# Retention chunks 0 to 5 turned in TensorE's transpose mode, their loads spread over three DMA queues, and another order of the first steps

## The chip, the cores and the metric

The kernel runs on one core of a Trainium2 chip. The metric is the device time of one execution in microseconds (us). The time before is a median of 667.78 us over 8 runs (666.61 to 669.93).

A core has five engines that run side by side, each with its own queue of instructions in a fixed order: TensorE (PE; its weight loads are listed apart as PEld), VectorE (DVE), ScalarE (ACT), GpSimd (POOL) and SyncE (SP). SP, ACT and POOL can issue DMA transfers between the chip's memory (HBM) and the on-chip buffers; a DMA that SP or ACT issues and one that POOL issues appear in the profile under different queues. An instruction that waits holds up everything behind it in its own queue.

## What is computed

The reference is a recurrent retention block (4 batches, 8 heads, 768 steps, head dimension 64), whose output is reshaped to 3072 x 512 and goes through a two-layer network with a quick GELU between:

```python
gamma = 1.0 - 2.0 ** (-5.0 - np.arange(H))
for t in range(S):
    state = gamma * state + einsum('bhd,bhe->bhde', k[:, :, t], v[:, :, t])
    y[:, :, t] = scale * einsum('bhd,bhde->bhe', q[:, :, t], state)
x = y.transpose(0, 2, 1, 3).reshape(B * S, H * D)      # 3072 x 512
h = x @ w_in                                           # 512 -> 2048
g = h * (1.0 / (1.0 + np.exp(-1.702 * h)))
out = g @ w_out                                        # 2048 -> 512
```

The two weights are handed to the kernel as raw 64-bit words (8 bytes for each value) and are narrowed to 32-bit floats on the chip.

## The kernel before, in words

**Retention.** The sequence is cut into chunks of 64 steps; two batches are worked on together (one in partitions 0 to 63, the other in 64 to 127), so there are 24 chunk steps j, 12 for each pair of batches. For a step, `load` (L125) brings q, k and v in tiles of 128 partitions x 8 heads x 64; `turn` (L239) makes the transposes of q and k; `turned` (L257) copies them out of PSUM on ACT; `attend(j, f)` (L280, called "step j-f") makes k·q products of chunk j (L288) and, for an earlier chunk f, the state's update (L296) and the output from the state (L305) and from the chunk itself (L311); `masked` (L315, DVE) applies the decay mask; `decay` (L262, ACT, eight instructions at L271) scales k; `by_state` and `output` (L320, L332, DVE) write the chunk into X; `aged` (ACT) and `updated` (DVE, L367) carry the state.

In steps 0 to 5 (`NEW = 6`) `turn` uses TensorE: 16 ordinary products of a 128 x 64 weight (two heads' halves go to the two halves of the output's partitions) with the identity matrix as the moving operand (L249). From step 6 on DVE's own transpose does it.

**The network.** X feeds products with w_in: the first two blocks (`up0` at L413, `up1` at L426), whose weights are narrowed while the kernel runs; later blocks use sums of weight and activation tiles that save products (L471, L575, L708).

**Narrowing a weight tile** ("w3" and so on, L180 to L220). SP fetches two 512 KB halves "b" and "a" into one of three raw buffers (`fetch`, L176, DMA at L178); ACT takes `abs` (L205); DVE does `half` (L209 to L211, 2.6 us for a full tile) and `rest` (L215 to L220, 3.2 us). A raw buffer is free for the tile after next but one when `rest` is done.

**The order.** PE's instructions stand in the order in which the program is written. On the other engines most of the first part is pinned to program order too. For the first stage that order is a list of words at L844 to L860, walked one after the other: `k0` is "load k of step 0", `turn0`, `w0b` is "fetch half b of weight tile 0", `abs0b`, `half0b`, `rest0b` narrow it, `step1` or `step5-4` is `attend`, `x0` writes the output of chunk 0, `up0.0.3` a product of the network, `gate0.0.3` its GELU, `warm` (L760) a product of the identity matrix with itself. `begin` (L749) comes ahead of the list; `rows` (L765), `mask` (L807), `causal` (L770, two instructions on POOL) build the decay mask, `whole` (L780) and `halves_anew` (L791) load and lay out decay factors. All DMAs of q, k and v are issued by SP, but k of step 0 by ACT. A tile of q, k or v has two buffers.

In the built program the DMAs of SP and ACT together take turns on eight completion semaphores, and those of POOL on eight others: a DMA waits until the one eight places ahead of it has landed.

```python
def plain(name, src, tag, bufs, engine=sp):                              # L133
    t = two.tile([P, H, D], F32, name=name + "_in", tag=tag, bufs=bufs)
    for i in range(2):
        if j < NEW:
            keep(engine.dma_start(t[i * D:(i + 1) * D], src[b + i, :, rows, :].rearrange("h p d -> p h d")))
...
for r in range(2):                                                       # L248
    pe.matmul(p[n][HALF[r], s, :], x[n][:, HP * r + s, :], ident, start=True, stop=True)
```

Of the kernel before, what the change touches and what calls it, by code (L numbers as in the profile page):

```python
# [9 lines left out]
F32 = mybir.dt.float32  # L10
U32 = mybir.dt.uint32
AF = mybir.ActivationFunctionType
ALU = mybir.AluOpType
P = 128
# [14 lines left out]
def kernel(  # L29
# [28 lines left out]
    nc = tc.nc  # L58
    pe, act, dve, pool, sp = nc.tensor, nc.scalar, nc.vector, nc.gpsimd, nc.sync
    ctx.enter_context(tc.manual_schedule(engines={mybir.EngineType.PE}))  # L60

    B, H, S, D = q.shape
    NT, DM = out.shape
    DFF = moe_w_in.shape[1]
    HP = H // 2
# [13 lines left out]
    one = ctx.enter_context(tc.tile_pool(name="one", bufs=1))  # L79
    two = ctx.enter_context(tc.tile_pool(name="two", bufs=2))  # L80
# [20 lines left out]
    rowd = const.tile([P, HP, D], F32, name="rowd")  # L101
    row = G[0:1, 4, 0:2].rearrange("p a (h t) -> p (a h) t", t=D)
    ones = G[0:1, 4, 2, 0:P]
    cold = const.tile([P, 2 * H], F32, name="cold")
    whole = const.tile([P, HP], F32, name="whole")
    whole_h = const.tile([P, H], F32, name="whole_h")
    ident = const.tile([P, P], F32, name="ident")
    mask = const.tile([P, 2, HP, D], F32, name="mask")
# [9 lines left out]
    def pin(i):  # L118
        return tc.keep_in_program_order(i) if ordered[0] else i


    NEW = 6
    QKV = {}

    def load(j, what="qkv"):  # L125

        b, c = j // NC * 2, j % NC
        rows = slice(c * D, (c + 1) * D)  # L130
        keep = tc.keep_in_program_order if j < 2 * CB else lambda i: i

        def plain(name, src, tag, bufs, engine=sp):  # L133
            t = two.tile([P, H, D], F32, name=name + "_in", tag=tag, bufs=bufs)
            QKV[name, j] = t
            for i in range(2):
                if j < NEW:
                    keep(engine.dma_start(t[i * D:(i + 1) * D], src[b + i, :, rows, :].rearrange("h p d -> p h d")))
                else:
                    for r in range(2):  # L140
                        keep(engine.dma_start(t[r * D:(r + 1) * D, i * HP:(i + 1) * HP],
                                              src[b + i, r * HP:(r + 1) * HP, rows, :].rearrange("h p d -> p h d")))

        if j < NEW:
            if "q" in what:
                plain("q", q, "q_sq", 2)
            if "k" in what:
                plain("kn", k, "k_sq", 2, sp if j else act)
        elif "q" in what:
            for name, src in (("q", q), ("k", k)):  # L150
                t = two.tile([P, H, D // C4, C4], F32, name=name + "_sq")
                for r0 in range(0, P, C4):
                    for n in range(D // C4):
                        t0 = c * D + n * C4
                        tc.keep_in_program_order(sp.dma_start(  # L155
                            t[r0:r0 + C4, :, n], src[b + r0 // D, :, t0:t0 + C4, r0 % D:r0 % D + C4]
                            .rearrange("h p d -> p h d")))
                QKV[name, j] = t
        if "v" in what:
            if j >= NEW and c < NC - 1:  # L160
                plain("kn", k, "kn", 1)
            plain("v", v, "v", 2)


    w1v = moe_w_in.bitcast(U32).rearrange("(c p) (f two) -> p c f two", p=P, two=2)
# [59 lines left out]
    QT, KT, KD, AT, TURNED, PA, PU, PY, SHARE = [{} for _ in range(9)]  # L225
    HALF = [slice(i * D, (i + 1) * D) for i in range(2)]
# [12 lines left out]
    def turn(j):  # L239

        QT[j], KT[j] = home(j, "qT"), home(j, "kT")
        if j < NEW:

            x = QKV.pop(("q", j)), QKV["kn", j]
            TURNED[j] = p = [ps.tile([P, HP, P], F32, name="pt", tag="y") for i in range(2)]
            for n in (1, 0) if j else (0, 1):
                for s in range(HP):
                    for r in range(2):  # L248
                        pe.matmul(p[n][HALF[r], s, :], x[n][:, HP * r + s, :], ident, start=True, stop=True)  # L249
        else:  # L250
            for t, name in ((QT[j], "q"), (KT[j], "k")):
                tc.keep_in_program_order(dve.transpose(
                    t.rearrange("p h t -> p (h t)"), QKV.pop((name, j)).rearrange("p h n d -> p (h n d)")))
        if 2 * CB <= j < NCH - 2:
            load(j + 2, "qk")
# [6 lines left out]
    def decay(j):  # L262

        if j % NC == NC - 1:
            return
        KD[j] = home(j, "kd")
        x = QKV["kn", j]
        if j < NEW:

            for h in range(H):  # L270
                pin(act.activation(KD[j][:, h], x[:, h], AF.Copy, scale=cold[:, H + h:H + h + 1]))  # L271
        else:
            pool.tensor_mul(KD[j].rearrange("p (i s) d -> p i s d", i=2), x.rearrange("p (i s) d -> p i s d", i=2),
                            cold[:, None, H:H + HP, None].to_broadcast([P, 2, HP, D]))
# [468 lines left out]
    W = col_decay.shape[1]  # L743
# [3 lines left out]
    works, products = {}, {}  # L747

    def begin():  # L749
        for i in range(2):  # L750

            pin(pool.dma_start(
                cold[HALF[i]].rearrange("p (n h) -> p n h", n=2),
                bass.AP(tensor=col_decay.tensor, offset=col_decay.offset, ap=[[W, D], [D * W + H, 2], [1, H]])))
        pin(pool.dma_start(row, row_decay[None, :, 0:D]))
        make_identity(nc, ident)
        dve.memset(ones, 1.0)
        dve.memset(first, 0.0)

# [27 lines left out]
    def late_loads():  # L787
        load(2 * CB, "qkv")
        load(2 * CB + 1, "qk")

    def halves_anew():  # L791

        pool.dma_start(whole_h, bass.AP(tensor=col_decay.tensor, offset=col_decay.offset + (D - 1) * W + H,
                                        ap=[[0, P], [1, H]]))
        pool.tensor_copy(mask[HALF[1], 0], mask[HALF[1], 1])
        pool.tensor_copy(cold[HALF[1], H:H + HP], cold[HALF[1], H + HP:2 * H])
        old, new = state[NEW % NC % 2], state[(NEW + 1) % NC % 2]
        for u in range(2):
            pool.dma_start(new[HALF[1 - u], u], old[HALF[u], 1 - u])
        for u in range(2):  # L800
            pool.tensor_copy(old[HALF[u], 1 - u], new[HALF[u], 1 - u])
# [20 lines left out]
    for name, i in [("0a", 0), ("0b", 1)] + [(str(p), 2 * p) for p in range(1, NFF)]:  # L822
        n = Narrow(i)
# [17 lines left out]


    begin()
    for name in """  # L844
        k0 table q0 warm turn0 w0b rows warm k1 abs0b q1 turned0 step0 v0 w0a half0b mask turn1 causal rest0b
        masked0 decay0 v1 decay1 abs0a half0a step-0 updated0 turned1 q2 step1 rowd k2 whole w2b turn2 w2a x0 k3
        aged1 masked1 turned2 v2 rest0a abs2 q3 step-1 updated1 state1 decay2 aged2 step2 q4 x1 half2 decay3 w3b
        w3a up0.0.0 masked2 turn3 k4 step-2 v3 q5 rest2 k5 gate0.0.0 turned3 updated2 state2 step3 up0.0.2
        masked3 abs3 half3 x2 rest3 turn4 w1b step-3 aged3 gate0.0.2 turned4 state3 w1a w5b updated3 v5 decay4
        abs1 x3 turn5 half1 up0.0.3 turned5 up0.1.2 step4 aged4 w5a rest1 v4 gate0.0.3 decay5 w6a masked4  # L850
        gate0.1.2 abs5 w6b step5-4 half5 rest5 up0.0.1 updated4 abs6 state4 gate0.0.1 w4b
        up0.1.1 half6 aged5 w4a up0.0.5 rest6 masked5 up0.1.5 gate0.1.1 x4 gate0.0.5 abs4 step-5 w8b w8a
        half4 gate0.1.5 state5 updated5 anew q6 up0.1.6 x5 rest4 gate0.1.6 abs8 v6 up0.0.6 w7b w7a half8
        turn6 gate0.0.6 up0.1.0 abs7 half7 gate0.1.0 w9b w9a up0.1.4 q7 gate0.1.4 decay6 step6 masked6 rest7 up0.0.4 v7
        gate0.0.4 turn7 up0.1.3 gate0.1.3 aged6 step7-6 masked7 updated6 decay7 abs9 state6 x6 up0.0.7 rest8 gate0.0.7
        w11a w11b step-7 state7 x7 half9 w10b w10a up0.1.7 rest9 gate0.1.7 abs11 half11 up1.8 gate1.8
        w12a w12b rest11 up1.5 gate1.5 up1.4 gate1.4 abs10 half10 up1.0 gate1.0 rest10 up1.3 gate1.3 abs12
        aged7 updated7 up1.2 gate1.2 w14b w14a half12 up1.6 gate1.6 rest12 up1.9 gate1.9 abs14 half14 w13a w13b
        up1.11 gate1.11 rest14 up1.10 gate1.10 abs13 half13 w15a w15b up1.7 gate1.7 rest13 abs15 half15 up1.12
        gate1.12 late_loads up1.13 gate1.13 rest15 up1.15 gate1.15 up1.14 gate1.14 up1.1 gate1.1  # L860
    """.split():
        works[name]()
# [93 lines left out]
```

## Time and profile before

| | |
|---|---|
| median of 8 runs | 667.78 us |
| the profiled execution | 669.93 us, of which the span is 668.2 us |
| mean granted TensorE clock | 0.995 |
| PE busy | 648.9 us (97% of the span) |
| DVE busy | 435.4 us (65%) |
| ACT, POOL busy | 148.8 us (22%), 176.2 us (26%) |
| the turn's products, L249 | 192 records on PE, 273 ns median each, from 6.4 to 44.2 us |
| one turn at full clock | 1.90 us on the chain of waits (at 31.25, 39.09 and 42.55 us) |
| loads of q, k, v of steps 0 to 5 | 12 DMAs each, 128 KB each |
| weight halves, 512 KB each | 5.7 us median from issue to landing (w_in into W) |

The page gives, for each engine, its busy time, then the span in 40 slices of 16.7 us (a digit is the busy share in tenths), then the DMA queues, then the chain of work that ended last, followed back from the end. The timeline lists instructions by start, with the idle time ahead of them and what ended it in brackets; a window query gives each engine's busy time, the granted clock, the DMA engines' busy share and GB/s in a stretch. Times are counted from the start of the span. A transfer's landing is read from the trace's completion events: each of 16 DMA engines reports once, and the transfer is complete with the last of the 16.

### The profile page before, as it was taken

The numbers are of one execution on the slowest core, as the hardware profiler recorded it, in microseconds if no ns is written. First come the engines' busy times: TensorE is split into PE (matmuls) and PEld (weight loads), VectorE is DVE, ScalarE is ACT, GpSimd is POOL, SyncE is SP. The second block draws the span as 40 slices with busy tenths as digits, with TensorE's granted clock in tenths as the row PEclk, the third lists the DMA queues.
The fourth block names the chain that finished last, engine by engine and source line by source line (L and its number), as shares of the span: only waits on it lengthen the run. The fifth ranks groups of instructions, "written<-read, shape, count | busy, mean of one in ns | idle before, by whom it ended". The sixth has DMA issues, their size and how long they took to land.

```text
span 668.2 us, 15234 instructions
## 1 busy us (share of the span) xinstructions
PE 648.9 (97%) x6438; PEld 563.3 (84%) x6438; DVE 435.4 (65%) x618; ACT 148.8 (22%) x285; POOL 176.2 (26%) x196
## 2 busy tenths in 40 slices
PE   6799989999999999999999899999999999999997
PEld 3788875446888888888999788999888999988997
DVE  3698778788545775456985254996264995254965
ACT  5664222231000000233100233110233110233110
POOL 3000310000268326100445600255700255500000
PEclk9799999999999999999999999999999999999999
DMA  9996557452203546263385652276662143502142
GB/s 182 218 228 182 144 106 233 153 98 33 47 10 134 172 111 181 60 224 123 88 216 126 206 143 94 73 178 174 176 177 95 61 148 112 221 32 94 51 157 94
DMA packets 150500, 89.49 MB, mean 134 GB/s; under 512 B 136192, under 2 KB 137472, under 8 KB 149408
## 3 DMA queue, kind: packets, MB, share of 16 engines
q1 hardware_dynamic: 140944, 46.50, 30.5%
q0 software_dynamic: 7184, 40.78, 17.0%
q10 hardware_dynamic: 2304, 1.25, 0.6%
q8 instruction: 50, 0.82, 0.5%
q14 instruction: 18, 0.15, 0.1%
HBM read 72.89 MB, written 15.47 MB: 132 GB/s over the span
## 4 chain that ended last, share of the span: by engine, by line
PE 83%; DMA 7%; SPq 3%; DVE 2%; POOL 2%; issue 1%; ACT 1%; POOLq 0%; DVEq 0%; ACTq 0%
PE pq L575 21%; PE px L471 16%; PE pd L708 13%; PE py L471 12%; PE ph L426 8%; PE ph L413 6%; DMA v_in<-in_v_dram 2%; DMA kn_in<-in_k_dram 2%; PE pa L288 2%; SPq L155 2%; PE pt L249 1%; PE pa L296 1%; PE py L311 1%; DMA W<-in_moe_w_out_dram 1%; PE py L305 1%
## 5 line engine op out<-in xcount | busy, mean ns | idle before, releaser
L575 PE MATMUL pq<-W,G 128*128 128x128 f32 x672 | 80.5, 276 | 0.1
L575 PEld LDWEIGHTS pq<-W,G 128*128 128x128 f32 x672 | 77.6, 192 | 0.9 <-issue 0.3
L544 POOL DMA_DIRECT2D ring<-W2D x28 | 15.4, 551 | 228.2 <-PE px L471 118.0
L471 PE MATMUL px<-X,W1A 128*128 128x256 f32 x256 | 60.0, 380 | 2.8 <-POOL X L441 2.8
L471 PE MATMUL px<-X,W1B 128*128 128x256 f32 x256 | 59.8, 379 | 0.0
L575 PE MATMUL pq<-ring,own 128*128 128x128 f32 x448 | 59.8, 276 | 0.0
L471 PEld LDWEIGHTS px<-X,W1A 128*128 128x128 f32 x256 | 48.2, 190 | 9.9 <-POOL X L441 3.6
L575 PEld LDWEIGHTS pq<-ring,own 128*128 128x128 f32 x448 | 54.5, 192 | 0.4
L471 PEld LDWEIGHTS px<-X,W1B 128*128 128x128 f32 x256 | 48.5, 190 | 6.7
L708 PE MATMUL pd<-W,G 128*128 128x256 f32 x224 | 49.6, 381 | 0.0
L708 PEld LDWEIGHTS pd<-W,G 128*128 128x128 f32 x224 | 42.2, 190 | 5.9
L471 PE MATMUL py<-X,W1A 128*128 128x256 f32 x192 | 45.4, 379 | 0.0
L471 PE MATMUL py<-X,W1B 128*128 128x256 f32 x192 | 45.4, 379 | 0.0
L392 ACT ACTIVATE G<-G 128x512 f32<-128x512 f32 x48 | 30.2, 630 | 52.0 <-DVE G L481 33.4
L471 PEld LDWEIGHTS py<-X,W1A 128*128 128x128 f32 x192 | 36.5, 190 | 5.0
L471 PEld LDWEIGHTS py<-X,W1B 128*128 128x128 f32 x192 | 36.5, 190 | 5.0
L489 DVE TENSOR_TENSOR t<-py,u 128x512 f32<-128x512 f32 x16 | 11.1, 692 | 35.3 <-PE py L471 35.3
L478 ACT ACTIVATE p<-px 128x512 f32<-128x512 f32 x16 | 9.6, 597 | 94.3 <-PE px L471 94.3
L575 PE MATMUL pq<-ring,G 128*128 128x128 f32 x224 | 29.6, 275 | 0.0
L575 PE MATMUL pq<-W,own 128*128 128x128 f32 x224 | 29.6, 275 | 0.0
L413 PE MATMUL ph<-X,W1B 128*128 128x256 f32 x128 | 29.0, 382 | 0.4 <-ACT X L392 0.4
L503 DVE TENSOR_TENSOR G<-G 128x512 f32<-128x512 f32 (+2 forms) x24 | 12.3, 513 | 25.7 <-ACT G L392 25.7
(206 smaller groups left out, 1163.4 us busy)
## 6 DMA issues: line engine op xcount, KB each, us to landing
ring<-W2D POOLq DMA_DIRECT2D x28, 768.0 KB, 5.0
W1B<-W1D POOLq DMA_DIRECT2D x6, 1792.0 KB, 9.5
W<-in_moe_w_in_dram SPq DMA_DIRECT2D x12, 512.0 KB, 5.7
W<-in_moe_w_out_dram SPq DMA_DIRECT2D x10, 512.0 KB, 5.5
out_dram<-o POOLq DMA_DIRECT2D x20, 256.0 KB, 3.5
q_sq<-in_q_dram SPq DMA_DIRECT2D x144, 32.0 KB, 2.4
k_sq<-in_k_dram SPq DMA_DIRECT2D x144, 32.0 KB, 2.4
v_in<-in_v_dram SPq DMA_DIRECT2D x72, 64.0 KB, 3.1
```

What stands on the lines that cost most here:

```text
L155: tc.keep_in_program_order(sp.dma_start(t[r0:r0 + C4, :, n], src[b + r0 // D, :, t0:t0 + C4, r0 % D:r0 % D + C4] .rearrange("h p d -> p h ...
L288: pe.matmul(pa[HALF[w], u, 0, s, :], kt[HALF[u], w, s, :], qt[HALF[u], w, s, :], start=True, stop=True)
L392: pin(act.activation(g, h[:, i], AF.Gelu_apprx_sigmoid))
L413: pe.matmul(h[:, ab], w, X[:, 2 * th + c // 2, c % 2, :], start=(ab == 0 and c == 0), stop=(c == 3), skip_group_check=True)
L426: pe.matmul(h, w, X1[:, c // 2:4:2, c % 2, :], start=(c == 0), stop=(c == 3))
L471: pe.matmul(acc[:, u, :], t[:, q1 + u, sa, c, :], X[:, sb, c, :], start=(start and u == 0 and c == 0), stop=(stop and c == 1), skip_group_ ...
L478: act.activation(p1, x, AF.Copy)
L489: dve.tensor_add(tt, z, u)
L503: dve.tensor_sub(q[0][1], q[0][0], q[0][1])
L544: pool.dma_start(c, W2D[i])
L575: pe.matmul(p0[:, j, :], a[:, d], w[:, d], start=(new and j == 0 and d == 0), stop=(d == NP // 2 - 1), skip_group_check=True)
L708: pe.matmul(p0[:, n, :], g1(m, p, sa)[:, n * P:(n + 1) * P], W2[:, sb, p, :], start=(new and p == 0 and n == 0), stop=(last and p == NP - ...
```

## The change

- `turn` in steps 0 to 5: 8 products in transpose mode, 128 x 128 each (two neighbouring heads at once), in place of 16 products of 128 x 64. So that neighbours are the right pair, q and k are loaded with heads 0 to 3 at the even places of the tile and heads 4 to 7 at the odd ones: four DMAs of 64 KB in place of two of 128 KB. `decay` reads the heads at their new places.
- k is loaded by ACT in step 0, by SP in step 2 and by POOL in steps 1, 3, 4, 5 (before: ACT in step 0, SP in the others). v of steps 0 to 5 is loaded by POOL (before: SP). q stays on SP.
- k of steps 2 and 3 takes the two buffers of the later output tile `o`; v of steps 2 and 3 those of two later scratch tiles (`s1`, `s2`), so that these four loads wait for no earlier step.
- In `begin`, POOL issues the load of `row`, makes the identity matrix and only then issues the loads of `cold`. The load of `whole_h` moves from about 3.4 us to its place in the list, behind all of POOL's other loads of this stage.
- The order of the first words: three `warm` and `rows` before `turn0`; `mask` and `causal` before `turned0`; `abs0b` and `half0b` behind `step0`; `k2` ahead of `v1` and `q2`; `updated0` ahead of `half0a`; `decay1` behind `turned1`; `v2` just behind `k3`.

```diff
 def plain(name, src, tag, bufs, engine=sp):
-    t = two.tile([P, H, D], F32, name=name + "_in", tag=tag, bufs=bufs)
+    if name == "v" and j in (2, 3):
+        t = one.tile([P, H, D], F32, name=name + "_in", tag=f"s{j - 1}")
+    else:
+        t = two.tile([P, H, D], F32, name=name + "_in", tag=tag, bufs=bufs)
...
-            keep(engine.dma_start(t[i * D:(i + 1) * D], src[b + i, :, rows, :].rearrange("h p d -> p h d")))
+            to, at = t[i * D:(i + 1) * D], src[b + i, :, rows, :].rearrange("h p d -> p h d")
+            for n in range(1 if name == "v" else 2):
+                keep(engine.dma_start(*((to, at) if name == "v" else (to[:, n:H:2], at[:, n * HP:(n + 1) * HP]))))
...
-        plain("kn", k, "k_sq", 2, sp if j else act)
+        plain("kn", k, "k_sq" if j in (0, 1, 4, 5) else "o", 2, {0: act, 2: sp}.get(j, pool))
...
-    plain("v", v, "v", 2)
+    plain("v", v, "v", 2, pool if j < NEW else sp)
...
 for s in range(HP):
-    for r in range(2):
-        pe.matmul(p[n][HALF[r], s, :], x[n][:, HP * r + s, :], ident, start=True, stop=True)
+    pe.matmul(p[n][:, s, :], x[n][:, 2 * s:2 * s + 2].rearrange("p r d -> p (r d)"), ident, is_transpose=True)
...
-    pin(act.activation(KD[j][:, h], x[:, h], AF.Copy, scale=cold[:, H + h:H + h + 1]))
+    pin(act.activation(KD[j][:, h], x[:, h % HP * 2 + h // HP], AF.Copy, scale=cold[:, H + h:H + h + 1]))
...
 def begin():
+    pin(pool.dma_start(row, row_decay[None, :, 0:D]))
+    make_identity(nc, ident)
     for i in range(2):
         pin(pool.dma_start(cold[HALF[i]]...
-    pin(pool.dma_start(row, row_decay[None, :, 0:D]))
-    make_identity(nc, ident)
...
-    pool.dma_start(whole_h, ...)
+    pin(pool.dma_start(whole_h, ...))
...
-    k0 table q0 warm turn0 w0b rows warm k1 abs0b q1 turned0 step0 v0 w0a half0b mask turn1 causal rest0b
-    masked0 decay0 v1 decay1 abs0a half0a step-0 updated0 turned1 q2 step1 rowd k2 whole w2b turn2 w2a x0 k3
-    aged1 masked1 turned2 v2 rest0a abs2 q3 step-1 updated1 state1 decay2 aged2 step2 q4 x1 half2 decay3 w3b
+    k0 table q0 warm warm warm rows turn0 w0b k1 q1 v0 mask causal turned0 w0a k2 step0 abs0b half0b turn1
+    masked0 rest0b decay0 v1 whole abs0a step-0 updated0 half0a turned1 decay1 q2 step1 rowd w2b turn2 w2a x0 k3
+    v2 aged1 masked1 turned2 rest0a abs2 q3 step-1 updated1 state1 decay2 aged2 step2 q4 x1 half2 decay3 w3b
```

Behind these lines the order is unchanged. Line numbers in the text are those of the kernel before.

## The prediction

> **What bounds the kernel now.** I read the page's slices first, then the chain of waits, then the first 60 us of the timeline.
>
> ```profile
> PE   6799989999999999999999899999999999999997
> DVE  3698778788545775456985254996264995254965
> PEclk9799999999999999999999999999999999999999
> ```
>
> PE is full from the third slice (33 us) on. The change edits nothing behind step 5, so its worth is how much earlier the later work gets under way. The chain of waits, of the stretch 14 to 60 us (start, length, what):
>
> ```profile
> 14.35 6.02 DMA kn_in<-in_k_dram
> ...
> 20.50 3.68 PE pt L249 x32
> ...
> 27.60 3.65 PE ph L413 x16
> 31.25 1.90 PE pt L249 x32
> ...
> 52.25 0.70 DVE G L317
> ```
>
> turn2 waits for k of step 2, which lands at 20.37. Two stretches of the next view explain the wait and the length of 3.68 (stretch, busy us of PE, PEld, DVE, ACT, POOL, then clock, DMA share, GB/s):
>
> ```profile
> 14.00:16.00 2.00, 1.34 (x68) 1.05 (x64) 1.18 (x3) 1.41 (x4) 0.47 (x1) 1.00 1.45 184
> 16.00:18.00 2.00, 0.25 (x9) 0.28 (x13) 1.56 (x3) 1.55 (x4) 0.00 (x0) 0.92 1.29 176
> 18.00:20.00 2.00, 0.88 (x32) 0.69 (x27) 1.03 (x3) 0.69 (x3) 0.00 (x0) 0.50 1.05 307
> 20.00:22.00 2.00, 1.50 (x14) 1.53 (x16) 1.38 (x2) 0.59 (x2) 0.00 (x0) 0.50 1.20 274
> ```
>
> The DMA engines are full (a share above 1.00 is overlap), and the clock is at half from about 18 to 24.6 us, behind a PE that idled. So the front is bound by transfers. Behind it DVE is the bound: from 27.32, where narrowing of tile w2 begins, to 50.57 it is busy 22.16 of 23.25 us. Then it waits for PE:
>
> ```profile
> 24.72 1.16 ACT L205 ACTIVATE W1A<-G 128x1024 f32<-128x1024 f32 x1
> 27.32 0.68 DVE L209 TENSOR_SCALAR W1A<-W1A 128x1024 f32<-128x1024 f32 x1
> 52.25 0.69 DVE L317 TENSOR_TENSOR G<-pa,mask 128x512 f32<-128x512 f32 x1 [1.67 <-PE pa L288]
> 53.29 0.69 DVE L209 TENSOR_SCALAR W1B<-W1B 128x1024 f32<-128x1024 f32 x1 [0.35 <-ACT W1B L205]
> 59.25 0.82 SPq L178 DMA_DIRECT2D G<-in_moe_w_out_dram  x2
> ```
>
> At 59.23 DVE frees a raw buffer; SP goes on at 59.25 and issues loads nearly without a pause until 91.8; step 7 starts on PE at 94.30. From 105.25 PE has 54.93 us of products in one piece. So I count the saving at **half5**, DVE's start at 53.29: all that follows hangs on PE and DVE, both full there, and shifts with it.
>
> **The turns.** Before: 32 records, 1.90 us at full clock. After: 8 transposes of 128 x 128. No row shows one. Upper bound: as an ordinary 128 x 128 product, two records of 114 ns (L575: 88 records in 10.02 us), 8 x 228 = 1.82 us. Lower bound: one record each at the shortest spacing of the trace (L288, 32 in 0.69 us, 22 ns), 8 x 22 = 0.17 us. I take one record of 114 ns each, as the row with the same tile is the nearest: 0.91 us, 1.0 us less per turn (bounds 0.1 to 1.7). The Trainium skill (TensorE: Matmul & The Clock Gate, Terms) calls transpose mode four times faster for FP32; a quarter of 1.90 would be an estimate of 0.48 us, 1.4 less per turn. turn0 and turn1 are hidden by transfers. turn3, 4 and 5 save PE 3.0 us between 31 and 44 us, but DVE is the bound there: this cover eats all but what PE owes DVE at 50.57 to 53.29.
>
> **The transfers.** Completion events of the trace (eighth of 16): k and q halves of 128 KB land 0.74 us apart (15.46, 16.21, 16.95), 1.47 us a load; the two halves of w2 at 19.80 and 21.36, 1.56 us a half. By 18.41 ten things had landed: k0 q0 k1 q1 v0 v1 q2 k2 and both halves of w0, 8 x 1.47 + 2 x 1.56 = 14.9 us of work in a row. Three queues make no byte less: in the stretch from 4 to 6 us, with SP's and ACT's queue at work, the trace gives 180 GB/s, against 184 at 14 to 16 with SP's alone. The same ten are due before turn2 in the new order (k2 earlier, q2 last). POOL's queue now runs ahead: v1 behind causal, then k3, v2, k4, v3, which wait for nothing late. I put half of k3 ahead of q2 (0.7 us): 19.1 for the eighth engine. The last engine trailed by 2.0 us before (20.37 against 18.41); with k2 no longer last I take 0.7: q2 at 19.8, between 18.4 and 21.4.
>
> PE then: turn2 at half clock 1.8, step-1 2.6 (1.8 before, partly at half clock), tmp and x1 on DVE 1.4 (25.99 to 27.40): x1 done at 25.6, against 27.40.
>
> half2 on DVE also needs w2a and its abs (1.16 us). Before, w2a's eighth engine landed at 21.36 and its last at 24.13. Ahead of it now stand k3 and v2 as well, 2.9 us, and some of k4: up to 25.2, plus a trailing engine. If packets of weights, which are larger, take turns with those of k and v one by one, the weights get more than half: only k3 and half of v2 ahead, 23.6. I take 25.0 with the last engine: abs done 26.2, **half2 at 26.3, 1.0 us earlier** (bounds: 3.4 earlier, with w2a at its old 21.36 and x1 at 23.8; 1.9 later, with w2a at 25.2 and its old trail of 2.8).
>
> w3 must not be late: half3 began at 36.12 and now would at 35.1. w3's halves landed by 34.85. With k4, v3 and some of k5 ahead (3.6 us) but k3, v2, and SP's pauses of 20.8 to 26.0 (5 us, waiting for buffers behind PE) gone, it lands at about 33.5: hidden.
>
> **What PE owes DVE.** At 50.57 DVE was done and stood 2.02 of the next 2.72 us: step 4 on PE came at 51.48, behind two blocks of products (44.4 to 51.5). The first of these needs rest3 (DVE, 42.5, now 41.5); PE, 2.0 us ahead by two turns and more, can start it at 41.6 in place of 44.4. step 4 then ends at about 49.4, before DVE asks (49.57). The abs of w5 on ACT, behind the GELU of the second block, ends about 50.4; half5 starts at 50.5. DVE gains 1.8 us here beyond the 1.0 (bounds 0 to 2.0).
>
> **POOL and ACT.** A DMA issue on POOL takes 0.52 us (64 rows of a tile) to 0.78 (256), so k costs 4 x 0.75 and v about 2 x 1.0: k1 3.9 to 6.9, v0 to 8.9, causal to 10.8 (before 11.62 to 13.46), v1 to 12.8, whole to 13.8, k3 to 16.8. Cover: nothing of these is asked for before step-0 (about 12.5). Queued behind a late mask would be causal, v1 and k3; behind k4, which waits for decay0, v3, k5, v5 and v4; none is due before 30 us. ACT issues two DMAs more, 1.6 us, under the wait for q0. The `rows` product now stands ahead of turn0; `row` was 6.2 us from issue to landing and is issued at 1.34: 5.2 to 7.5, the third `warm` ends at about 5.6. turned1 is behind abs0a, thus behind w0a (14.64, the same seven transfers ahead), as before.
>
> **Sum.** 1.0 + 1.8 = 2.8 us. The profiled execution took 669.93 (span 668.2, 1.73 around it): 667.1. The median of the runs is 2.15 below it: **665.0 us**.
>
> **Rivals.**
> - *The weights come late* (slower). POOL's early k3, v2, k4 and v3 take DMA time ahead of w2 in full: 21.36 + 4 x 1.47 = 27.2, and the old trail of 2.8 makes 30.0. half2 at 31.2 is 3.9 later; less 1.8 it is 2.1 slower: 669.9. It decides from w2a landing at 27.9. For it: POOL's queue waits for nothing late. Against: POOL issues a quarter load per 0.75 us, and before, 512 KB halves overtook a second queue (w0b, issued at 2.26, landed at 8.58; k0's second half, issued at 1.58, at 8.32).
> - *The clock stays at half.* PE has less work between 8 and 20 us, and transposes are shorter. If turn2, step-1 (3.6) and the first block (7.3 in place of 3.65) all run at half, x1 comes at 26.9, PE is 1 us behind before at 35 and 1 ahead at 44: gain 0.3 + 0.7 = 1.0, 666.8. For it: the clock fell behind 2 us of thin work. Against: it rose again 4 us after turn2 began. The Trainium skill (TensorE: Matmul & The Clock Gate, Part 4) says that transposes do not count as a busy PE for the gate; if so, release waits for step-1 and the loss is this rival's; no row of this trace has a transpose.
> - *Transposes cost what the turns did* (1.82 us). Then PE is no more ahead than by the 1.0 of half2, and the 1.8 shrinks to about 0.3: 1.3 in all, 666.5.
> - *The weights are not hurt* and q2 lands at 18.4: 3.4 + 2.0 = 5.4, 662.4.
>
> **Chances.** Forecast 0.50, large gain 0.14, weights late 0.16, clock 0.10, dear transposes 0.10. 0.2% (1.3 us) is about what a measurement of this kernel can tell from no change. Faster by more: 0.50 + 0.14 + half of the dear transposes = 0.69; within: 0.15; slower: 0.16. The range goes from the large gain less the spread of runs (1.2 to 2.2, half the difference of lowest and highest being 1.7): 662.4 - 1.7 = 660.7, to just under the slow rival, 669.6.
>
> **What would show it.** After: L249's successor at 8 transposes of about 0.9 us a turn; turn2 starting near 19.8; the first L209 on a full tile near 26.3; half5 near 50.5 with no wait for L288 ahead of it; PE's 55-us piece starting near 102.4. I am wrong if the full-tile L209 starts after 27.3, or if DVE's lead is lost between 59 and 105, where I let everything shift.

## The result and the profile after

The changed kernel takes 672.4 us (median of 11 runs, 671.47 to 679.42) against 667.8 us before: a ratio of 1.0091, interval 1.0072 to 1.011. It is slower; 665.0 was forecast. The profiled execution took 676.49 us (span 674.8, mean clock 0.982), so it stands 4.1 above its median, where that of before stood 2.15 above; so the two profiles lie 6.6 us apart and the medians 4.6.

The slices of the page, after (PE, DVE, clock):

```profile
PE   6769999999999999999999999999999999999997
DVE  3658967879455686265987254897254896254965
PEclk8779999999999999999999999999999999999999
```

PE is full only from the fourth slice (50 us) on, one slice later than before; the clock is down in the third as well. The chain of waits of after, 5 to 64 us (start, length, what):

```profile
7.15 9.95 DMA W<-in_moe_w_in_dram
...
17.12 0.60 SPq L143
...
18.41 9.75 DMA G<-in_moe_w_in_dram
...
29.40 0.70 DVE W1A L214
...
30.11 12.97 DMA W<-in_moe_w_in_dram
...
44.36 0.70 DVE W1A L214
...
51.58 8.06 PE ph L417 x32
```

Three weight halves now carry it: those of w0, w2 and w3 land at 17.11, 28.16 and 43.09. Before, they landed at 14.64, 24.13 and 34.85. (Lines of after are four or five higher: L214 is `half`, L210 `abs`, L417 `up0`, L253 the turn, L143 the loads of q, k, v, L183 the weights.) The timeline, with DVE's and ACT's waits:

```profile
28.24 1.12 ACT L210 ACTIVATE W1A<-G 128x1024 f32<-128x1024 f32 x1 [3.15 <-DMA G<-in_moe_w_in_dram]
29.40 0.69 DVE L214 TENSOR_SCALAR W1A<-W1A 128x1024 f32<-128x1024 f32 x1 [0.96 <-ACT W1A L210]
...
43.17 1.16 ACT L210 ACTIVATE W1A<-W 128x1024 f32<-128x1024 f32 x1 [7.37 <-DMA W<-in_moe_w_in_dram]
44.36 0.69 DVE L214 TENSOR_SCALAR W1A<-W1A 128x1024 f32<-128x1024 f32 x1 [5.98 <-ACT W1A L210]
...
60.33 0.69 DVE L321 TENSOR_TENSOR G<-pa,mask 128x512 f32<-128x512 f32 x1 [1.93 <-PE pa L292]
61.37 0.69 DVE L214 TENSOR_SCALAR W1B<-W1B 128x1024 f32<-128x1024 f32 x1 [0.35 <-ACT W1B L210]
```

| | before | after | later by |
|---|---|---|---|
| half2 on DVE (w2) | 27.32 | 29.40 | 2.1 |
| half3 on DVE (w3) | 36.12 | 44.36 | 8.2 |
| half5 on DVE | 53.29 | 61.37 | 8.1 |
| PE's 55-us piece | 105.09 | 112.92 | 7.8 |
| end of the span | 668.2 | 674.8 | 6.6 |

The whole loss is made by 44.36, at half3; of the 8.2 us, 1.6 come back by the end of the span. DVE, which was to be the bound, waits 5.98 us for w3. The turn itself is as cheap as forecast (timeline of PE, after):

```profile
32.05 0.60 PE L253 MATMUL pt<-ident,kn_in 128*128 128x128 f32 x4
32.48 0.60 PE L253 MATMUL pt<-ident,q_in 128*128 128x128 f32 x4
```

Each of the eight transposes has one record; the next product starts at 33.01, so a turn takes 0.96 us at full clock (1.90 before, 0.91 forecast). The clock is worse: 0.50 from 14 to 26 us, against about 18 to 24.6 before. The DMA engines are as full. The first of these stretches (stretch, busy us of PE, PEld, DVE, ACT, POOL, then clock, DMA share, GB/s):

```profile
14.00:16.00 2.00, 1.75 (x32) 1.45 (x36) 1.65 (x3) 0.00 (x0) 1.25 (x3) 0.50 1.24 195
```

Two things delay w3. First, SP issues it later: 29.49 and 30.11 in place of 26.77 and 27.44. SP's queue, before and then after:

```profile
20.80 5.87 SPq L138 DMA_DIRECT2D q_in<-in_q_dram  x4
26.77 1.32 SPq L178 DMA_DIRECT2D W<-in_moe_w_in_dram  x2
```

```profile
18.98 9.79 SPq L143 DMA_DIRECT2D q_in<-in_q_dram  x8
29.49 0.99 SPq L183 DMA_DIRECT2D W<-in_moe_w_in_dram  x2
```

q of steps 3 and 4 are now eight DMAs. The eighth takes the completion semaphore of w2's second half, so it waits until that has landed (28.16) and is issued at 28.18. The halves of w3 in their turn take the semaphores of the first two DMAs of q of step 3, which landed at 29.43 and 30.05. In the same way the last DMA of q of step 2 waited for w0 (issued 17.12, the first lines of the chain), and behind it SP issued w2's second half at 18.41, 2.7 us later than before (15.70).

Second, w3 takes longer once issued: 12.97 us for its second half, against 7.4 before (27.44 to 34.85). 2.7 later and 5.6 longer are the 8.2. POOL's queue is what stands beside it: packets, MB and share of the 16 engines by queue, of the stretch 30 to 44 us, after:

```profile
q1 hardware_dynamic: 2846, 2.36, 79.8%
q0 software_dynamic: 368, 0.82, 31.0%
```

q0 is POOL's queue, q1 that of SP and ACT. At the 230 GB/s of this stretch the 0.82 MB are an estimated 3.6 of the 5.6 us. While w2 was under way POOL's share was larger still; the stretch 24 to 29 us, after and then before:

```profile
q0 software_dynamic: 242, 0.60, 67.6%
q1 hardware_dynamic: 1048, 0.34, 52.2%
```

```profile
q1 hardware_dynamic: 2240, 0.60, 58.6%
```

POOL's loads (v of step 2, first used at 33.01, then k of step 4, used at 42.4, and v of step 3) got 0.60 of 0.94 MB there, while w2's second half was unfinished until 28.16 and the weights received some 0.10 MB (50 records of 2048 bytes). In the records POOL's loads are 4096 bytes each (354 ns mean), SP's q 256 bytes (36 ns).

### The profile page after: what moved, and what is told of

The parts are those of the page before. It is cut to its first block, busy times and chain, and to the rows that moved or that the text cites. A ratio compares the mean times of both kernels' runs of the same rounds, so it can differ in the third digit from the quotient of the medians.

```text
span 674.8 us, 15002 instructions
## 1 busy us (share of the span) xinstructions
PE 649.5 (96%) x6296; PEld 562.9 (83%) x6296; DVE 434.4 (64%) x618; ACT 148.1 (22%) x285; POOL 193.8 (29%) x224
## 3 DMA queue, kind: packets, MB, share of 16 engines
q1 hardware_dynamic: 130608, 43.88, 27.9%
## 4 chain that ended last, share of the span: by engine, by line
PE 84%; DMA 8%; DVE 4%; SPq 2%; POOL 1%; issue 1%; ACT 0%; POOLq 0%; ACTq 0%; DVEq 0%
PE pq L579 24%; PE px L475 16%; PE pd L712 13%; PE py L475 12%; PE ph L430 8%; PE ph L417 4%; DMA W<-in_moe_w_in_dram 3%; PE pa L292 2%; PE py L315 1%; DMA G<-in_moe_w_in_dram 1%; PE py L309 1%; DMA W<-in_moe_w_out_dram 1%; PE pa L300 1%; SPq L143 1%; DMA k_sq<-in_k_dram 1%
## 5 line engine op out<-in xcount | busy, mean ns | idle before, releaser
L475 PEld LDWEIGHTS py<-X,W1B 128*128 128x128 f32 x192 | 36.5, 190 | 5.0
L475 PEld LDWEIGHTS py<-X,W1A 128*128 128x128 f32 x192 | 36.5, 190 | 5.0
L417 PE MATMUL ph<-X,W1A 128*128 128x256 f32 x128 | 31.4, 404 | 1.1 <-DVE X L350 1.1
L417 PEld LDWEIGHTS ph<-X,W1A 128*128 128x128 f32 x128 | 25.9, 205 | 5.2 <-DVE X L350 1.2
```

Of the source, the lines that this page charges most:

```text
L417: pe.matmul(h[:, ab], w, X[:, 2 * th + c // 2, c % 2, :], start=(ab == 0 and c == 0), stop=(c == 3), skip_group_check=True)
L475: pe.matmul(acc[:, u, :], t[:, q1 + u, sa, c, :], X[:, sb, c, :], start=(start and u == 0 and c == 0), stop=(stop and c == 1), skip_group_ ...
```

## The experiments

**Theory A:** k and v on POOL's queue put bytes of later steps ahead of the weights. **Theory B:** the doubled number of DMAs on SP delays the weights in SP's own queue (about 0.65 us an issue, and a ring of eight semaphores that now spans two loads of q or k in place of four). **Rivals:** the transposes themselves or the clock; the new order. Ratios are to the kernel before, run on the same chip in the same session (medians 668.05, 667.37, 667.07 and 667.33 us in the four sessions); a ratio is not the quotient of the medians, which for the changed kernel is 1.0069. half1, half2, half3 and half5 are DVE's starts on w1, w2, w3 and w5; w1 comes behind w3.

### Which part does it: four cuts of the change

e1, the changed kernel with POOL's loads on SP:
```diff
-plain("kn", k, ..., {0: act, 2: sp}.get(j, pool))
+plain("kn", k, ..., {0: act}.get(j, sp))
-plain("v", v, "v", 2, pool if j < NEW else sp)
+plain("v", v, "v", 2)
```


> The changed kernel with every load that it had moved to POOL (k of steps 1, 3, 4, 5, v of steps 0 to 5) given back to SP; transpose mode, the four DMAs for q and k, the extra buffers and the new order stay. Theory A, POOL's queue: its 4096-byte packets (16 pieces of 256 bytes, 359 ns each in the trace of after) win the DMA engines from SP's 256-byte (31 ns) and 2048-byte packets (115 ns), so the weights come late; without it the second half of w3 lands near 35 us (after 43.1, before 34.9), the first full-tile half starts near 27, half5 near 52 (after 61.4, before 53.3): 666.5, ratio 0.998 (0.994 to 1.001). Theory B, transposes and the clock: the granted clock stays at half until 27 us and again at 36 to 41 and the time stays near 671. Theory C, the new order and the doubled number of DMAs: near 671 too.

672.74 us, 1.0072 (1.0047 to 1.0097); half2 26.9, half3 40.0, half5 58.2. Without POOL's loads w2 is early, yet SP issues w3 at 30.98, and the loss stays. Theory A alone falls.

e2, the kernel before with k of steps 1, 3, 4, 5 and v of steps 0 to 5 on POOL, and nothing else:
```diff
-plain("kn", k, "k_sq", 2, sp if j else act)
+plain("kn", k, "k_sq", 2, {0: act, 2: sp}.get(j, pool))
-plain("v", v, "v", 2)
+plain("v", v, "v", 2, pool if j < NEW else sp)
```


> The kernel before with one edit: k of steps 1, 3, 4, 5 and v of steps 0 to 5 are issued by POOL (two DMAs a load, two buffers each, old order, old turns). Theory A: slower than before, though a little less than after, since without the extra buffers POOL's queue waits for steps and cannot run ahead so far: 670.5, ratio 1.004 (1.001 to 1.009), with the second half of w3 landing after 37 us. Theories B and C: 667.8, within 0.2% of before.

671.27 us, 1.0034 (1.0011 to 1.0058); half2 28.2, half3 40.0, half5 57.6. So POOL's queue alone costs too, but not as expected: w3 was issued at 25.77 and landed at 34.42, no later than before. PE was late: it stood 2.25 us on "issue" ahead of 29.40 and then ran the first block in 5.35 us at a lowered clock (3.72 at full).

e3, the kernel before with the transposes and their four DMAs, all on SP (the hunks of `plain`, `turn` and `decay`):
```diff
+for n in range(1 if name == "v" else 2):
+    keep(engine.dma_start(*((to, at) if name == "v" else (to[:, n:H:2], at[:, n * HP:(n + 1) * HP]))))
...
+pe.matmul(p[n][:, s, :], x[n][:, 2 * s:2 * s + 2].rearrange("p r d -> p (r d)"), ident, is_transpose=True)
...
+pin(act.activation(KD[j][:, h], x[:, h % HP * 2 + h // HP], AF.Copy, scale=cold[:, H + h:H + h + 1]))
```


> The kernel before with the turns alone changed: transpose mode, q and k loaded by four DMAs of 64 KB, the heads' new places in decay; all loads on SP (k of step 0 on ACT), old order, old buffers. Theory A: no harm, a turn at full clock takes 0.9 to 1.1 us in place of 1.90 and the DVE's wait of 1.67 us at 50.6 shrinks: 666.3, ratio 0.998 (0.995 to 1.001). Theory B (transposes cost the clock): 670 or more. If the doubled number of DMAs on SP is the harm: 669 or more, with SP's queue never idle ahead of the weights.

673.61 us, 1.0079 (1.0049 to 1.0109); half2 27.5, half3 40.0, half5 58.2. The turns were cheap and x1 was done at 25.5 (forecast 25.6), but w3 was issued at 31.46 and w1 at 44.19; ACT's abs waited 4.97 and 5.39 us for them.

e4, the changed kernel with these three hunks undone, so with the ordinary turn and two DMAs:
```diff
+keep(engine.dma_start(t[i * D:(i + 1) * D], src[b + i, :, rows, :].rearrange("h p d -> p h d")))
...
+pe.matmul(p[n][HALF[r], s, :], x[n][:, HP * r + s, :], ident, start=True, stop=True)
```


> The changed kernel with the old turns (ordinary products of 128 x 64, two DMAs of 128 KB for each q and k, heads in order); three queues, extra buffers and the new order stay. Theory A: as slow as after or slower by up to 1.5 us: 672.5, ratio 1.007 (1.003 to 1.011), w3 landing after 40 us. Theory B: the harm goes with the transposes, 668 or less.

673.13 us, 1.0075 (1.0048 to 1.0103); half2 27.3, half3 41.6, half5 57.4. Here w3 was issued early, at 22.46 and 25.62, and landed at 38.15 and 40.38: 15 us for each 512 KB, beside POOL's k and v. That is theory A at its plainest. The timeline of ACT shows the wait:

```profile
40.47 1.15 ACT L208 ACTIVATE W1A<-W 128x1024 f32<-128x1024 f32 x1 [3.10 <-DMA W<-in_moe_w_in_dram]
```

PE also stood 5.64 us on "issue" (23.24 to 28.87). Each of e1, e3 and e4 costs about what the whole change does: two causes, each enough for the loss, and they do not add up. Both end at the same place, DVE's wait for w3. The new order is not a third: e1 and e3 differ in the order and the extra buffers alone, and their ratios are 1.0072 and 1.0079. No run has the new order by itself.

### The doubled DMAs without the transposes, and the reverse

e9, four DMAs with the ordinary turn, all on SP, old order (e3's hunks of `plain` and `decay`, and):
```diff
-pe.matmul(p[n][HALF[r], s, :], x[n][:, HP * r + s, :], ident, ...)
+pe.matmul(p[n][HALF[r], s, :], x[n][:, 2 * s + r, :], ident, ...)
```


> The kernel before; q and k of steps 0 to 5 come in four DMAs of 64 KB instead of two of 128 KB, all from SP as before (k of step 0 from ACT), heads at the interleaved places; the turn is the ordinary products of before. Theory B (each DMA costs SP about 0.6 us whatever its size; the doubled number holds up w3 and w1 behind q and k): as slow as the kernel with transposes and four DMAs on SP alone: w3 issued by SP at about 31 us (26.8 before), half3 at about 40, half5 near 58, 673 us +-1.5. Rival (the transposes themselves or the clock did the harm there): w3 issued within 1 us of before, 667 to 669 us.

674.84 us, 1.01 (1.0068 to 1.0132); half3 39.4, half1 52.1, half5 58.5. The queue of SP in this kernel:

```profile
25.16 7.01 SPq L140 DMA_DIRECT2D q_in<-in_q_dram  x8
32.27 1.06 SPq L180 DMA_DIRECT2D W<-in_moe_w_in_dram  x2
```

w3 is issued 5.5 us later than before, w1 at 44.81 in place of 37.40. Splitting the loads, with not one transpose in the kernel, costs 1%: theory B holds, and the transposes are not needed for the loss.

e10, transposes of neighbouring heads, loads as before:
```diff
-for r in range(2):
-    pe.matmul(p[n][HALF[r], s, :], x[n][:, HP * r + s, :], ident, start=True, stop=True)
+pe.matmul(p[n][:, s, :], x[n][:, 2 * s:2 * s + 2].rearrange("p r d -> p (r d)"), ident, is_transpose=True)
```


> The kernel before; the turn is 8 transposes of two neighbouring heads, but the loads stay two DMAs of 128 KB with the heads in their plain order. The heads thereby land at other places than the later steps take them for, so the result is that of a permuted computation; the work is the same in kind and amount. This is the pure effect of the transpose mode, without its loads. Forecast of the prediction: about 1 us less per turn, half5 at DVE about 2 us earlier than 53.3 (50.5 to 52), 665 to 667 us. Rival (transposes lower the granted clock and the first products give back what the turns save): half5 at 53 to 54, 668 to 670 us. A time of 672 or more would mean that theory B is not the cause of the loss with transposes alone.

665.3 us, 0.9977 (0.9953 to 1.0001); half2 25.3, half3 35.0. DVE's timeline around half5:

```profile
49.81 0.68 DVE L316 TENSOR_TENSOR G<-pa,mask 128x512 f32<-128x512 f32 x1
50.41 0.68 DVE L209 TENSOR_SCALAR W1B<-W1B 128x1024 f32<-128x1024 f32 x1
```

half5 starts at 50.41 with no wait for PE ahead of it: the prediction had 50.5 and 665.0 us. Against its own session's 667.37 the mode alone is worth about 2 us, though the interval just reaches no change. A kernel that keeps these loads and carries the other places of the heads through mask, state and output was not tried.

### POOL's share of it

e12, the changed kernel with v back on SP:
```diff
-plain("v", v, "v", 2, pool if j < NEW else sp)
+plain("v", v, "v", 2)
```


> The changed kernel with v of steps 0 to 5 back on SP; k stays on POOL, the order, the buffers and the transposes stay. Theory A plus B: POOL's queue moves half the bytes, so w0, w2 and w3 land earlier than in the changed kernel (w3 by 39 in place of 43), half3 at 38 to 41, 669 to 671.5 us. Rival (the new order is what delays, whatever the queue): half3 at 43 or later, 672 to 674 us.

669.74 us, 1.0025 (1.0004 to 1.0047); half2 30.7, half3 39.3, half5 56.0. With half of POOL's bytes gone, half3 is 5 us earlier than in the changed kernel and the ratio falls from 1.0091 to 1.0025. w2 did not land earlier, as was expected, but at 29.48, and w3 was issued later than in the changed kernel, at 32.04 and 32.69. The gain is all in w3's own way: 4.94 us for its second half in place of 12.97.

e6, the changed kernel without the extra buffers:
```diff
-if name == "v" and j in (2, 3):
+if False:
...
-"k_sq" if j in (0, 1, 4, 5) else "o"
+"k_sq"
```


> The changed kernel with k and v of steps 2 and 3 back in the two old buffers, so that POOL's loads of these steps wait for steps 0 and 1 again; queues, transposes and order stay. If the prefetch is what puts POOL's bytes ahead of w2 and w3 (theory A in its narrow form): w2 lands before 27 (28.2 in the changed kernel), w3 before 40 (43.1), half3 at 38 to 42, 669 to 671.5 us. Rival (it is the queue itself: k and v on POOL beside SP, with or without the extra buffers): w3 lands at 41 or later, half3 at 42 or later, 671.5 to 674 us.

671.55 us, 1.0066 (1.0043 to 1.0089); half2 27.3, half3 37.6, half1 49.5, half5 57.1. w2 and w3 landed at 26.05 and 36.32, as the narrow form of theory A says, and the time is just above what it expected, since w1 is now the late one:

```profile
36.41 1.15 ACT L210 ACTIVATE W1A<-W 128x1024 f32<-128x1024 f32 x1 [2.72 <-DMA W<-in_moe_w_in_dram]
48.38 1.13 ACT L210 ACTIVATE W1A<-W 128x1024 f32<-128x1024 f32 x1 [6.05 <-DMA W<-in_moe_w_in_dram]
```

The extra buffers decide which weight tile the early loads push back; in both cases POOL's queue pushes one back.

e15 and e16, the kernel before with 512 KB more of v that nothing reads, issued by POOL or by ACT:
```diff
+for n in range(2):
+    t = two.tile([P, H, D], F32, name="extra", tag="o", bufs=2)
+    for i in range(2):
+        pin(pool.dma_start(t[i * D:(i + 1) * D], v[2 + i, :, n * D:(n + 1) * D, :].rearrange("h p d -> p h d")))
...
-k2 whole w2b turn2
+k2 whole extra w2b turn2
```


> The kernel before and four DMAs more of 128 KB (512 KB of v, into buffers that nothing reads until much later), issued by POOL just behind the load of whole, at about 14.5 to 17.3 us, so beside the loads of k2 and w2 that SP issues. Nothing else differs. Theory A (loads of POOL's queue, in 4096-byte packets, take more than their share from SP's queue beside them): k2 or w2's second half lands 2 to 3 us later than before, half2 on DVE at 28.5 to 30.5 (27.3 before), most of the 2.8 us that 512 KB take at 190 GB/s; 668.5 to 671 us. Rival (queues share the DMA engines evenly): half2 within 1.2 us of before, 667 to 669 us.

> The same four DMAs more of 128 KB, issued by ACT at the same place of the order (about 17 to 19.6 us, behind rowd). The bytes are the same, the queue is ACT's, whose packets are 256 bytes. Theory A: the small packets take less from w2's 2048-byte packets, so w2 is hardly later than before and the extra loads themselves are slow: half2 at 27.3 to 28.3, earlier than with POOL by 1 us or more; 667 to 669.5 us (ACT's issues, 2.6 us, stand ahead of x0 and the aged state). Rival (only the bytes count): half2 as late as with POOL within 0.5 us.

POOL 672.96 us, 1.0095 (1.0067 to 1.0123); ACT 668.88 us, 1.0023 (1.0005 to 1.0042). The mechanism expected was not seen: half2 starts at 27.1 in both. With POOL, SP had issued w2 (14.80 and 15.46) ahead of the first extra load (16.56), and w2 landed at 22.95. With ACT the extra loads came first, from 14.43; w2 was issued at 15.78 and 17.20 and landed at 25.85. Some 3 of the 4 us between the two come through PE. Its timeline with POOL, then with ACT:

```profile
25.75 0.56 PE L288 MATMUL pa<-G 64*64 64x64 f32 x19
29.26 0.69 PE L288 MATMUL pa<-G 64*64 64x64 f32 x12 [2.96 <-issue]
29.88 5.04 PE L413 MATMUL ph<-X,W1A 128*128 128x256 f32 x16
```

```profile
27.62 0.45 PE L288 MATMUL pa<-G 64*64 64x64 f32 x12 [2.32 <-issue]
28.00 3.72 PE L413 MATMUL ph<-X,W1A 128*128 128x256 f32 x16
```

PE stops in the middle of one group of products, waits for nothing that another engine does, and goes on 1.6 us later with POOL; then the clock is at half and the block takes 1.3 us more. half5 is at 57.0 and 53.8. This is the same stop as in e2 and e4 (see the last section). So the experiment does not settle whether the size of POOL's packets matters; that these loads cost more on POOL's queue than on ACT's is measured, but they were not issued at the same moment, and the reason in this pair is PE's stop and the clock behind it.

### Attempts at a better kernel

e11, transposes with four DMAs, old order, old buffers, k of steps 1, 3, 4, 5 on POOL, v on SP (e3's edits and):
```diff
+plain("kn", k, "k_sq", 2, {0: act, 2: sp}.get(j, pool))
```


> The kernel before with transposes and four DMAs, but k of steps 1, 3, 4, 5 issued by POOL; q and all v on SP; old order, old buffers. SP then issues about as many DMAs as before and POOL carries half the bytes that it does in the changed kernel. Theory A plus B: SP's queue is no longer late (w3 issued by 27), POOL's large packets cost the weights little since only 256 KB a step go that way; half3 at 36 to 38, half5 at 53 to 55.5, 667 to 670 us. If the number of DMAs on SP is not the point but POOL's queue is (A alone): still near 671. Rival (transposes hurt by the clock): 671 or more with w3 landed by 36.

668.93 us, 1.0013 (0.9995 to 1.003); half3 38.2, half5 53.5. No change, as A and B together expect; w3 was issued at 28.42, not by 27, behind eight q DMAs that took 7.07 us.

e13, e11 with w3 moved:
```diff
-step2 q4 x1 half2 decay3 w3b w3a up0.0.0
+step2 w3b w3a q4 x1 half2 decay3 up0.0.0
```


> The kernel with transposes and four DMAs on the old order, k of steps 1, 3, 4, 5 on POOL, and one move more: SP issues both halves of w3 before q of step 4 instead of behind it. Theory B (SP's queue of 0.6 us a DMA is what makes w3 late): w3 is issued at 24 to 25 us instead of 28.4, DVE starts half3 at about 36 instead of 38.2 with no wait for ACT ahead of it, half5 at 51 to 53, 665.5 to 667.5 us, faster than before. Rival (w3 is late by what else the DMA engines carry, not by its place in SP's queue): half3 stays at 37.5 or later, 668 to 670 us.

667.58 us, 1.001 (0.9996 to 1.0024); half2 29.4, half3 38.0, half5 54.7. The expectation missed: w3 was issued at 26.54 and 28.22, not by 25, because the fourth DMA of q3 held SP for 1.96 us in place of 0.61 and the second half waited for a half of w2 (28.16), eight places ahead. Even so w3 landed at 34.72 and half3 did not wait for it. Now w2 was late: it was issued at 18.96 and 19.61 (before: 15.03 and 15.70), half2 waited for it, and half3 follows half2 by 8.5 us (8.8 before). PE also stood 2.46 us on "issue" ahead of 23.25.

e14, e3 with w3 and w1 moved:
```diff
-step2 q4 x1 half2 decay3 w3b w3a up0.0.0
+step2 w3b w3a q4 x1 half2 decay3 up0.0.0
...
-v3 q5 rest2 ... turn4 w1b step-3 ... state3 w1a w5b
+v3 w1b w1a q5 rest2 ... turn4 step-3 ... state3 w5b
```


> The kernel with transposes and four DMAs all on SP, old order, but SP issues w3 before q of step 4 and w1 before q of step 5. Theory B: what the doubled DMAs cost was only that they stood ahead of w3 and w1; then w3 is issued at about 25 (31.5 without the move) and w1 by 36 (44.2), half3 at 35 to 36.5, half1 at 44 to 46, half5 at 51 to 53.5, 666 to 668.5 us. Rival: with all on SP the queue is simply too long, and k and q of steps 4 and 5 are late in the weights' place: PE waits for kn_in or q_in before turn4 or turn5, half5 at 55 or later, 670 us or more.

673.69 us, 1.0104 (1.0072 to 1.0136); half3 36.5 and half1 46.0, 3.5 and 5 us earlier than in e3 though w3 was issued at 28.84 and not at 25, but half5 58.7. The rival was right, PE pays (its timeline):

```profile
47.29 0.94 PE L250 MATMUL pt<-ident,kn_in 128*128 128x128 f32 x4 [5.06 <-DMA kn_in<-in_k_dram]
```

With split loads SP's queue is too long in total; another order only chooses who is late.

e17, only k turned by transposes and split, on POOL as in e11; q as before:
```diff
+for n in range(1 if name != "kn" else 2):
...
+if n:
+    pe.matmul(p[n][:, s, :], x[n][:, 2 * s:2 * s + 2].rearrange("p r d -> p (r d)"), ident, is_transpose=True)
+    continue
```


> The kernel before; only k is turned by transposes and loaded in four DMAs, those of steps 1, 3, 4, 5 by POOL; q keeps two DMAs of 128 KB on SP and its ordinary products; v stays on SP; old order, old buffers. SP now issues two DMAs a step less than before. Theory B (SP's number of DMAs makes w3 late): w3 is issued by 25.5 and DVE's half3 does not wait for it, it starts at 34.5 to 36; half of the turns' saving remains, half5 at 51 to 53, 665.5 to 667.5 us. Rival (POOL's 256 KB a step take the DMA engines from w3, or PE's code comes late again, whatever SP issues): w3 lands after 34.5, or PE stands 2 us or more on issue, half5 at 54 or later, 668.5 to 671 us.

670.6 us, 1.0043 (1.0022 to 1.0063); half3 38.9, half5 58.1. The rival again: w3 was issued at 26.55 and landed at 36.19, and PE stood on "issue" (the block behind this line took 6.56 us):

```profile
37.48 0.71 PE L293 MATMUL pa<-G 64*64 64x64 f32 x16 [2.24 <-issue]
```

None of these four versions was measurably faster than the kernel before.

## Why the prediction was wrong

- **The turns: right.** 0.96 us a turn against 0.91, and alone (e10) 665.3 us against 665.0, half5 at 50.41 against 50.5. The rival of dear transposes is out. That e10 meets the whole forecast is partly luck: the forecast's first term (1.0) was to come through the new order's transfers, which e10 does not have, and against its own session it gains 2.1 us, not 2.8. Transpose mode was to be four times faster by the Trainium skill (TensorE: Matmul & The Clock Gate, Terms); in these kernels a turn is 1.98 times faster.
- **"Three queues make no byte less ... the same ten are due before turn2 in the new order ... q2 at 19.8": failed first.** The working counted bytes, and issues only on ACT and POOL. That q's loads became four DMAs was priced nowhere on SP, although a DMA waits for the one eight places ahead. q of step 2 was released by w0's landing (17.11) and PE waited for it until 23.38.
- **"A trailing engine ... 25.0" for w2: failed.** It landed at 28.16, past the 27.9 from which the slow rival was to decide. That rival had the direction and the tile's lateness, but only part of the mechanism: of the 4.0 us that w2 landed later than before, 2.7 are its later issue behind q of step 2 and 1.3 its longer way. POOL's loads show earlier, at w0, whose second half was issued sooner than before (7.15, 8.98) and landed later (17.11, 14.64). The rival's price for half2 was too high (29.40, not 31.2), and it had none for w3, which lost 8.2.
- **"If packets of weights, which are larger, take turns ... the weights get more than half": failed.** The weights' records are larger than SP's (2048 bytes against 256), but not than POOL's (4096). POOL's loads got 64% of the bytes between 24 and 29 us, and in e4 w3 took 15 us. The Trainium skill (DMA: Bandwidth & Descriptors, Queues, rings and completion order) says that an engine takes turns between queues packet by packet. That agrees with a larger share for POOL's larger records, but no run here changes the packet size alone.
- **"w3 lands at about 33.5: hidden": the step that cost most.** It took 3.6 us of other loads ahead of w3 and removed SP's pauses. SP's pauses did not go, they grew (9.79 us for the eight q DMAs), and w3 was issued 2.7 us later and took 5.6 us longer. At 35.1 DVE was to be free; 44.36 is when it started. The pauses were also misread: of the two before, the one up to 25.99 ended with PE's work, the one up to 23.69 with nothing that the trace shows.
- **The 1.8 that PE owed DVE: not gained.** From half3 to half5 it is 17.0 us, before 17.2. The turn of step 5 and the block behind it ran at half clock (1.90 and 8.06 us; before 1.90 with the old turn, and 7.10), and DVE waited for PE as before (1.93 us, 1.67 before).
- **"Everything shifts": right, but for 1.6 us.** 8.2 at half3 is 7.8 at PE's 55-us piece and 6.6 at the end.
- **The clock rival: in part.** The half clock lasted from 12.8 to 26.5 us (17.7 to 24.5 before) and came back from 36.7 to 40.1 and from 47.0 to 53.8, each time with a wait of PE (1.94 us ahead of 36.58, 3.66 us ahead of 47.70). In e10, where the loads are as before, PE ran at half speed until 15.9 us (two `warm` products took 2.08 us at 10.74; before, 1.13 at 10.53) and again from 22.7 to 29.5, behind a stop of 1.89 us. e9 and e15, with ordinary turns, came to full clock even later, at 19.2 and 18.9. So no run here separates whether transposes count as work for the clock gate.

## What to carry to other kernels

Price a split load on the queue that issues it: here each DMA held SP for about 0.65 us whether it moved 64 or 128 KB, and with a ring of completion semaphores twice as many DMAs halve the depth in loads; e9, which changes only the loads and the places of the heads, lost 1%. A second queue adds no bandwidth where the engines are full (195 GB/s with POOL's queue and 184 without it between 14 and 16 us): what it fetches early is taken from what the first queue needs now, so look which transfer is due first. Where a change needs two edits (a mode and the layout it asks for), measure or price each alone: here the mode alone was worth about 2 us, at the edge of what was measurable, and the layout cost 7.5 (e9).

## What the runs showed of the hardware that was not expected

PE stops where no wait shows, and the times point at its own code. In nine executions PE stands on "issue" inside or between groups of products, by 0.64 us (before) to 5.64 us (e4), and each time it goes on 1.4 to 2.0 us after the end of a 16,384-byte packet of the instruction queue: 25.57 and 27.16 before, 27.61 and 29.40 in e2, 27.32 and 28.87 in e4, 27.71 and 29.26 in e15, 26.17 and 27.62 in e16, 36.08 and 37.48 in e17, with e9, e10 and e13 alike. In before, e2, e15 and e16, whose PE programs are the same, it is the same place: twelve products are left of a group of 32. These packets share the 16 DMA engines with the loads. That PE waits for them, and that they are late because the engines are full, is argued, not shown: the trace does not tell whose they are or when they were asked for, and the other seven executions have such packets and no such stop. What follows can cost more than the stop: behind it the clock stood at half in e2, e4, e10, e15 and e17, and the block of 3.72 us took 5.04 to 6.56 us there; before and in e16 it took 3.72.
